# RWKV6 attention and a tanh-shrink feed-forward layer: joining a second pair of steps in blocks 3 to 5, with forms of weights kept in device memory

## The chip, the cores and the metric

The kernel runs on one core of a Trainium2 chip. The metric is the device time of one execution in microseconds (us). The engines are named as in the profile: PE (TensorE, matrix products, with PEld for its weight loads), DVE (VectorE), ACT (ScalarE), POOL (GpSimd) and SP (SyncE, which issues most DMAs). Each engine works through its own program in order; semaphores tie the programs together.

## The reference

```python
batch, n_heads, seq, head_dim = (4, 8, 768, 48)
for t in range(S):                       # attention, one state of 48 x 48 for each head
    cur = einsum('bhd,bhe->bhde', u[None] * k[t], v[t])
    y[t] = einsum('bhd,bhde->bhe', r[t], state + cur)
    state = w[t][..., None] * state + einsum('bhd,bhe->bhde', k[t], v[t])
x = y.transpose(0, 2, 1, 3).reshape(3072, 384)
h = x @ w_in                             # 384 -> 2048
g = h - tanh(h)
out = g @ w_out                          # 2048 -> 384
```

All inputs and outputs are float32.

## The kernel before

The 3072 tokens are cut into eight blocks of 384 (four batches, two halves each). A block is a loop over 16 steps `f` (L1355), each one slice of 128 of the 2048 inner features. While block i does its feed-forward layer, the attention of block i+1 (`later`) is prepared, and inputs of block i+2 (`after`) are loaded. PE, SP, DVE and ACT run in the order in which the code is written (`manual_schedule`), so that the position of a line is its place in the engine's queue.

**One single step.** `first` (L886) multiplies the block's tokens `xT` by the step's slice of `w_in`: three 128x128x384 products into the bank `hp`, which the profile shows as six rows of L888. ACT copies the result to `h` (L893). `slight` (L967) then has ACT form `s` (the square), `qa` and `junk` (a check of the range, called `over`), and leaves two products for DVE (L896), which run in the next step as `rest`. They give a slice of `g`.

**The second layer.** Two steps make a pair q. Its 384x256x384 product is done by `Fewer` (L1078) with fewer multiplications, from sums and differences of parts of g (`form_g`, L1009; DVE rows of L1013) and of `w_out`. `form_g` runs over the following steps: forms 0 and 2 as `formed`, 4, 6 and 8 as `forming`, or `carried` to a later step around a joined pair. The products of a pair go to PE in two parts (`Fewer.add`, twelve rows of L1092 each), the first two steps after the pair's end, the second three; the list `due` holds them. Three more products of each pair, `others` (L1106), go to a bank of `ps_a`; for pairs 0 to 3 that is in step 9. The pieces are put together in the next block by `SUMS` (DVE rows of L1127), in the steps that the dictionary `some` (L1388) names.

**A joined pair.** For the pairs in `JOINED` (L122) the two steps share their first product. `Twos.begin` (L938) makes it from 11 products of 128x128x192 (22 rows of L951) into the two tiles of `ps_a`. It needs five forms of the weights (`weight_forms`, L919, DVE rows of L927) and four forms of the tokens (`token_forms`, L930, DVE rows of L935). ACT copies one part out (L952), and four DVE additions (`outs`, rows of L961) give h of both steps. `begin` and `outs` stand in the even step; `slight` follows there for the first h, and in the odd step for the second. Blocks 3 to 6 join pair 1 (steps 2 and 3), block 6 also pair 7, block 7 pairs 0 to 6.

**Room on the chip.** The forms and results of a joined pair lie in tiles whose contents are not needed just then (`spare_tile`, L899): pair 1 uses `v_sb` and `late` for its forms and `ks` for its results. A tile taken this way is written only when its last reader is done.

**The attention of the next block**, by steps as `plan` (L1146) gives them for blocks 3 to 6: `split` (ACT) writes 16-bit planes into tile `w` in step 2; `turned` (L547) is a DMA transposition from `w`, in step 4 to `ks` and in step 5 to `post`; `join` (ACT rows of L555) puts the words together again in `ks`: one copy each in steps 6, 7 and 8, three in step 9. `update` (PE rows of L578, step 10) reads `ks`, in the order of head pairs 3, 2, 1, 0 for four chunks of tokens and then the same for the last two; the three copies of step 9 belong to head pairs 1 and 0. It is followed by the updates of the states on DVE (L590, step 11), and `results` (PE rows of L774, step 12). `product_u`, `product_r` and `product_sum` (DVE) stand in steps 5, 6 and 7, `diagonal_in` in 8 and 9. The loads of the block after next stand at steps 7 (`w`), 9 (`k`) and 11 (`r`); `bound` (ACT, L459) and `behind` (DVE scan) read the new `w` from step 10 on.

**DVE's order within a step** is one list, such as this one for the even step of a joined pair beyond the first:

```python
ops = between(rest, carried) + outs[:1] + formed + outs[1:] + spare
```

`between` interleaves two lists; `spare` holds the sums, the preparation of the next block and the forms for joined pairs.

Of the kernel before, what the change touches and what calls it, by code (L numbers as in the profile page):

```python
# [37 lines left out]
F32 = mybir.dt.float32  # L38
# [13 lines left out]
P = 128  # L52
L = 64
NB = 384
NQ = S // NB
NCH = NB // L
NCP = NCH // 2
NPAIR = H // 2
# [7 lines left out]
DM = H * D  # L66
FF = 2048
KC = DM // P
NF = FF // P
# [44 lines left out]
SUMS = (("sub", (15, 6, 10), (0, 0, 6)), ("sub", (2, 2, 5), (3, 5, 3)),  # L114
        ("add", (6, 7, 13), (1, 7, 1)), ("add", (7, 9, 14), (5, 9, 11)),
        ("sub", (10, 10, 14), (5, 5, 6)), ("add", (11, 12, 11), (10, 2, 10)),
        ("sub", (14, 4, 14), (11, 3, 11)), ("add", (2, 8, 13), (10, 5, 10)),
        ("add", (13, 4, 13), (2, 2, 15)), ("add", (8, 8, 12), (4, 4, 12)),
        ("add", (0, 4, 0), (11, 2, 11)), ("sub", (14, 14, 1)))
PLACES = ((8, 10, 0), (2, 5, 13), (11, 7, 14))  # L120
TWOS = range(7)
JOINED = {3: (1,), 4: (1,), 5: (1,), 6: (1, NF // 2 - 1), 7: TWOS}  # L122


SLIGHT = 2.0 ** -6
# [4 lines left out]
def kernel(  # L130
# [12 lines left out]
    nc = tc.nc  # L143
# [3 lines left out]
    work = ctx.enter_context(tc.tile_pool(name="work", bufs=2))  # L147
# [42 lines left out]
    def draw(names, cols):  # L190
        nc.gpsimd.memset(mask_all[0:L, cols], 1.0)
        for m in names:
# [5 lines left out]
            else:  # L198
# [10 lines left out]
                   in_=start[:, 0:BANK].unsqueeze(1).to_broadcast([P, 2 * NPAIR * NCP * L // BANK, BANK]))  # L209
# [107 lines left out]
    def begin_behind(ins, then):  # L317
        tc.add_manual_dep(then.ins, ins.ins.name, mybir.DependencyInfo(
            mybir.DependencyClass.Sync, mybir.DependencyReason.DATA))
# [579 lines left out]
    def spare_tile(name, width=2 * HALF, pool=inp):  # L899
        return pool.tile([P, width], F32, name=name, tag=name, bufs=1)  # L900
# [245 lines left out]
    def plan(i):  # L1146


        formed_w = {}
        if i == 0:  # L1150
            phases = {6: ("turn",), 7: ("update",), 10: ("earlier",), 13: ("results",)}
            before = {0: ("behind 2", "take_whole 2"), 2: ("behind 0", "take_whole 0"), 3: ("times_behind 2",),
                      4: ("times_behind 0",), 5: ("before 2",), 6: ("before 0",), 7: ("times_before",),
                      9: ("product_u", "held", "bound 2"), 10: ("product_r", "bound 0"), 11: ("product_sum",), 12: ("diagonal_in 2", "diagonal_in 0")}
            ahead = {}
            loads = {f: "weights" for f in (0, 1, 3, 4, 5, 6, 7, 8, 9, 10)}
            loads.update({2: "next r", 11: "w", 13: "k", 14: "r"})
            loads = {f: [name] for f, name in loads.items()}
            loads[3] += ["v", "row"]
            loads[4] += ["tokens k"]  # L1160
            loads[9] += ["tokens r"]
        else:
            phases = {3: ("split 2 0",), 4: ("earlier", "split 2 1", "turned 2", "split 0 01"), 5: ("turned 0",),
                      6: ("join 2 0",), 7: ("join 2 1",), 8: ("join 2 2",), 9: ("join 0 02",), 10: ("update",),
                      12: ("results",)}
            before = {0: ("times_behind 2",), 1: ("times_behind 0",), 3: ("times_before", "held"),
                      5: ("product_u",), 6: ("product_r",), 7: ("product_sum",), 8: ("diagonal_in 2",),
                      9: ("diagonal_in 0",)}
            ahead = {10: ("bound 2", "bound 0"), 11: ("behind 2", "take_whole 2"), 12: ("behind 0", "take_whole 0"),
                     13: ("before 2",), 15: ("before 0",)}  # L1170
            loads = {1: ["v"], 3: ["tokens k"], 4: ["tokens r"], 7: ["w"], 9: ["k"], 11: ["r"]}
            if i in JOINED:
                before.update({2: ("times_before",), 3: ("held",)})
                phases.update({3: (), 4: ("earlier", "turned 2")})
                loads = {3: ["tokens k"], 4: ["tokens r"], 5: ["v"], 7: ["w"], 9: ["k"], 11: ["r"]}
        if i == 1:
            phases = {4: ("split 2 0",), 5: ("split 2 1", "turned 2"), 6: ("split 0 01",),
                      7: ("earlier", "turned 0", "join 2 0"), 8: ("join 2 1",), 9: ("join 2 2", "join 0 01"),
                      10: ("join 0 2",), 11: ("update",), 13: ("results",)}
            before = {0: ("behind 2", "take_whole 2", "bound 2"), 1: ("behind 0", "take_whole 0"),  # L1180
                      2: ("times_behind 2",), 3: ("before 2", "bound 0"), 4: ("times_behind 0",), 5: ("before 0",),
                      6: ("times_before", "held"), 7: ("product_u",),
                      9: ("product_r", "product_sum", "diagonal_in 2"), 10: ("diagonal_in 0",)}
            ahead = {12: ("bound 2",), 13: ("behind 2", "take_whole 2"), 14: ("bound 0",)}
            loads = {1: ["v"], 4: ["tokens k"], 6: ["tokens r"], 9: ["w"], 11: ["k"], 12: ["r"]}
            formed_w = {2: (0, 1), 7: (2, 3, 4, 5), 9: (6,), 10: (7, 8), 11: (9,), 12: (0, 1), 13: (2, 3, 4, 5, 6),
                        14: (7, 8, 9)}
        elif i == 2:
            phases.update({3: (), 4: ("split 2 0",), 5: ("earlier", "split 2 1", "turned 2", "split 0 01"),
                           6: ("turned 0", "join 2 0")})  # L1190
            before = {0: ("behind 0", "take_whole 0", "times_behind 2"), 1: ("times_behind 0",), 2: ("before 2",),
                      3: ("before 0",), 4: ("times_before", "held"), 5: ("product_u",), 7: ("product_r",),
                      8: ("product_sum",), 9: ("diagonal_in 2", "diagonal_in 0")}
            loads = {1: ["v"], 3: ["tokens k"], 5: ["tokens r"], 8: ["w"], 10: ["k"], 11: ["r"]}
        return phases, before, ahead, loads, formed_w
# [1 line left out]
    blocks = [Block(b, q) for b in range(B) for q in range(NQ)]  # L1197
    manual = ExitStack()
    manual.enter_context(tc.manual_schedule(engines={PE, SP, DVE, ACT}))
    raws = []  # L1200

    def more_weights(queue):
        raws.append(load_weights(more_weights.n, queue))
# [141 lines left out]
    for i, blk in enumerate(blocks):  # L1345
        here = xT
# [8 lines left out]
        for f in range(NF):  # L1355
# [8 lines left out]
            if not joined:  # L1364
                h, made = first(here, f, to[:, 0:NB], SPACED[i][f > 12 + (i < 2)])
            elif f % 2 == 0:
                for op in behind:
                    op()
                behind = []
                by = beside if near else twos  # L1370
                outs = by.begin(ps_a, f // 2)
                if near:
                    for name in ("split 2 0", "split 2 1", "split 0 01"):
                        later.phase(ps_a, name)
            if not i:
# [9 lines left out]
                    op()  # L1385
            else:
                ahead_of_h, square = [], []
            some = ({4: (0, 2), 6: (2, 4), 8: (4, 6), 9: (6, 8), 14: (8, len(SUMS))} if after else  # L1388
                    {4: (0, 2), 6: (2, 4), 8: (4, 6), 9: (6, 8), 11: (8, 10), 12: (10, len(SUMS))} if later else
                    {4: (0, 1), 5: (1, 2), 6: (2, 3), 7: (3, 4), 8: (4, 5), 9: (5, 9), 10: (9, 11),  # L1390
                     11: (11, len(SUMS))}).get(f) if summed else None
# [4 lines left out]
                              if of and not name.startswith("bound")]  # L1396
            if i:
                spare += [lambda n=n: form_w(n, 4 if f < 12 else 6, 2) for n in formed_w.get(f, ())]
            if later and i in JOINED and f < 2:
                if not f:  # L1400
                    beside, v_left, late_left = (Twos(1, 1), spare_tile("v_sb", NCP * DM), spare_tile("late", NB))
                    for x in range(5):
                        beside.form(x, v_left, x * P)
                    beside.results(spare_tile("ks", NPAIR * NCP * P, work))
                    spare += beside.weight_forms(0, 2, 1, 4, 3)
                else:
                    spare += beside.token_forms(here, beside.halves((v_left, 5 * P), (late_left, 0)))
            if i == blocks_n - 2:
                if f == 10:
                    twos = Twos(0, NF // 2)  # L1410
# [107 lines left out]
            for name in loads.get(f, ()):  # L1518
                of, ins = (after if name in ("w", "k", "r") else later), None
                if name == "weights":  # L1520
                    ins = more_weights(nc.sync)
                elif name == "row":
                    ins = nc.sync.dma_start(out=u_row, in_=u_all)
                elif of and name.startswith("tokens"):
                    ins = of.load_tokens(name[-1])
                elif of:
                    ins = of.load_v() if name == "v" else of.load(name.split()[-1])
                if ins:
                    begin_behind(made, ins)
            if f < 2 and summed:  # L1530
                summed[0].others(ps_a, ((4, 5, 6), (7,))[f], None if later else hp)
                if f:
                    behind.append(summed[0].others_summed)
# [95 lines left out]
```

## Time and profile before

| | before |
|---|---|
| median of 3 runs | 541.09 us (540.89 to 542.05) |
| profiled execution, own time | 540.57 us |
| its span, first to last instruction | 538.7 us |
| PE clock granted in it | 0.998 |
| DVE groups: form_g L1013, sums L1127 | 106.6 us in 270, 33.0 us in 84 |
| ACT groups: qa L980, junk L984 | 69.6 us in 113, 68.0 us in 113 |
| DMA moved | 56.36 MB, mean 105 GB/s |

A row of a timeline gives start, duration, engine, line, operation, output and inputs, and how many instructions were merged; a bracket gives the idle time before it and what ended it. PE rows of a timeline overlap by about 0.16 us because products are pipelined; the chain that ended last gives them end to end. Two engine rows that overlap on DVE or ACT do so in the same way.

### The profile page before, as it was taken

How to read it: one execution, taken by the hardware profiler on the slowest of the kernel's cores; microseconds unless marked ns; L12 is line 12 of the kernel's file. 1: busy time of each engine (PE TensorE's matmuls, PEld its weight loads, DVE VectorE, ACT ScalarE, POOL GpSimd, SP SyncE). 2: the span in 40 equal slices, each digit the busy share in tenths (PEclk: the TensorE clock that was granted, in tenths of full speed). 3: DMA queues.
4: the chain of work that ended last, by engine and by line, in shares of the span. 5: the costliest groups of instructions: out<-in, count | busy, mean ns of one | idle time of the engine just before them, and what ended most of it. 6: DMA issues, size and time to landing. Idle time of an engine off the chain costs nothing.

```text
span 538.7 us, 15161 instructions
## 1 busy us (share of the span) xinstructions
PE 529.3 (98%) x5820; PEld 419.7 (78%) x5820; DVE 495.9 (92%) x1044; ACT 393.4 (73%) x796; POOL 9.2 (2%) x57
## 2 busy tenths in 40 slices
PE   7999999999999999999999999999999999999996
PEld 5756665677777777877878787787878877999993
DVE  7999999999989989999898989989899899979885
ACT  4999986988668876678676787587865886546460
POOL 1100000000000000000000000000000000000001
PEclk9999999999999999999999999999999999999999
DMA  8798742252311632164211632128232340100011
GB/s 279 244 408 327 237 122 72 101 136 65 121 32 65 163 109 59 53 116 150 63 56 46 149 119 66 51 60 192 63 90 68 47 103 16 43 2 1 10 36 47
DMA packets 53049, 56.36 MB, mean 105 GB/s; under 512 B 21488, under 2 KB 50928, under 8 KB 52976
## 3 DMA queue, kind: packets, MB, share of 16 engines
q1 hardware_dynamic: 52592, 55.18, 34.8%
q8 instruction: 49, 0.80, 0.6%
q14 instruction: 24, 0.20, 0.1%
q10 hardware_dynamic: 288, 0.10, 0.1%
q0 software_dynamic: 96, 0.07, 0.1%
HBM read 44.73 MB, written 4.72 MB: 92 GB/s over the span
## 4 chain that ended last, share of the span: by engine, by line
PE 95%; DVE 2%; DMA 1%; PEld 1%; issue 0%; ACT 0%; SPq 0%; PEldq 0%; DVEq 0%
PE hp L888 36%; PE acc L1092 27%; PE att L951 8%; PE att L1092 6%; PE acc L1043 5%; PE att L774 4%; PE att L497 2%; PE att L578 1%; PE acc L1070 1%; PE att L888 1%; DMA r<-in_rT 1%; PE acc L888 1%; PE hp L1092 0%; PE att L520 0%; DVE scores L505 0%; DVE pre L420 0%
## 5 line engine op out<-in xcount | busy, mean ns | idle before, releaser
L888 PE MATMUL hp<-xT,w_sb 128*128 128x384 f32 x594 | 208.8, 488 | 0.5 <-DVE w_sb L271 0.5
L888 PEld LDWEIGHTS hp<-xT,w_sb 128*128 128x128 f32 x594 | 106.3, 190 | 57.0 <-issue 0.6
L1092 PE MATMUL acc<-forms,g 128*128 128x128 f32 x972 | 136.0, 276 | 0.0
L1092 PEld LDWEIGHTS acc<-forms,g 128*128 128x128 f32 x972 | 124.4, 192 | 7.7
L1013 DVE TENSOR_TENSOR g<-g 128x256 f32<-128x256 f32 x270 | 106.6, 419 | 0.7 <-PE acc L1092 0.2
L893 ACT ACTIVATE h<-hp 128x384 f32<-128x384 f32 x99 | 48.5, 490 | 75.4 <-PE hp L888 75.3
L980 ACT ACTIVATE qa<-s,shift 128x384 f32<-128x384 f32 x113 | 69.6, 616 | 3.7
L984 ACT ACTIVATE junk<-s,shift 128x384 bf16<-128x384 f32 x113 | 68.0, 601 | 0.4
L896 DVE SCALAR_TENSOR_TENSOR h<-h,s 128x384 f32<-128x384 f32 x104 | 57.1, 549 | 11.7 <-ACT s L979 11.6
L1092 PE MATMUL acc<-w_sb,g 128*128 128x128 f32 x324 | 54.1, 276 | 0.0
L1092 PEld LDWEIGHTS acc<-w_sb,g 128*128 128x128 f32 x324 | 47.0, 192 | 7.6 <-ACT sums L1060 0.3
L896 DVE SCALAR_TENSOR_TENSOR g<-qa,h 128x384 f32<-128x384 f32 x88 | 48.4, 550 | 1.3
L979 ACT ACTIVATE s<-h 128x384 f32<-128x384 f32 x89 | 46.6, 523 | 2.8
L1127 DVE TENSOR_TENSOR sums<-sums 128x256 f32<-128x256 f32 x84 | 33.0, 409 | 1.2 <-ACT sums L1104 1.0
L1043 PE MATMUL acc<-w_sb,sums 128*128 128x384 f32 x96 | 33.7, 487 | 0.0
L1092 PE MATMUL att<-w_sb,g 128*128 128x128 f32 x200 | 33.4, 275 | 0.0
L267 ACT ACTIVATE up<-raw 128x768 f16<-128x768 f32 (+1 forms) x32 | 33.1, 1076 | 0.0
L1092 PEld LDWEIGHTS att<-w_sb,g 128*128 128x128 f32 x200 | 29.0, 192 | 4.2
L1043 PEld LDWEIGHTS acc<-w_sb,sums 128*128 128x128 f32 x96 | 18.0, 190 | 12.3 <-DVE sums L896 0.3
L420 DVE TENSOR_TENSOR_SCAN pre<-w,start 128x780 f32<-128x780 f32 x14 | 25.0, 1783 | 0.8
L951 PE MATMUL att<-xT,w_sb 128*128 128x192 f32 x120 | 25.4, 326 | 0.0
L432 DVE TENSOR_TENSOR_SCAN post<-w,seed 128x780 f32<-128x780 f32 x14 | 24.9, 1776 | 0.0
(185 smaller groups left out, 715.2 us busy)
## 6 DMA issues: line engine op xcount, KB each, us to landing
raw<-in_weights SPq DMA_DIRECT2D x16, 768.0 KB, 6.7
w<-in_wT SPq DMA_DIRECT2D x7, 780.0 KB, 4.5
k<-in_kT SPq DMA_DIRECT2D x7, 768.0 KB, 5.2
r<-in_rT SPq DMA_DIRECT2D x7, 768.0 KB, 4.6
v_sb<-in_v SPq DMA_DIRECT2D x8, 576.0 KB, 4.7
k<-in_tokens SPq DMA_DIRECT2D x7, 576.0 KB, 3.9
r<-in_tokens SPq DMA_DIRECT2D x7, 576.0 KB, 4.9
out_y<-sums SPq DMA_DIRECT2D x18, 128.0 KB, 1.9
```

The lines of the kernel that those rows point to most:

```text
L267: return lambda: nc.scalar.activation(out=to, in_=of, func=AF.Copy, scale=scale, bias=bias)
L888: nc.tensor.matmul(hp, lhsT=w_in_sb[:, f, kc, :], rhs=xT[kc], start=(kc == KC - 1), stop=(kc == 0))
L893: return h, nc.scalar.activation(out=h, in_=hp, func=AF.Copy, scale=1.0 / UPSCALE)
L896: return lambda: nc.vector.scalar_tensor_tensor(out=out, in0=in0, scalar=scalar, in1=in1, op0=op0, op1=ALU.mult)
L951: nc.tensor.matmul(to, lhsT=lhs, rhs=rhs, start=n == 0, stop=n + 1 == len(of))
L979: nc.scalar.activation(out=s, in_=h, func=AF.Square, scale=scale)
L980: nc.scalar.activation(out=qa, in_=s, func=AF.Square, bias=shift[:, 4:5])
L984: nc.scalar.activation(out=junk[:, 0:NB], in_=s, func=AF.Relu, bias=shift[:, 5:6], accum_out=excess[:, at:at + 1])
L1013: return lambda: nc.vector.tensor_tensor(out=G[:, to:to + 2], in0=two(G, g_at(q, a0), g_at(q, a1)), in1=two(G, g_at(q, b0), g_at(q, b1)), ...
L1043: nc.tensor.matmul(acc, lhsT=g[:, j * P:(j + 1) * P], rhs=w_out_sb[:, f, :], start=(f == self.first), stop=(f == NF - 1))
L1092: nc.tensor.matmul(to, lhsT=G[:, g_at(q, a), :], rhs=rhs, start=start, stop=stop, skip_group_check=True)
L1127: ops.append(lambda op=op, at=at: nc.vector.tensor_tensor(out=at[0], in0=at[1], in1=at[2], op=OPS[op]))
```

## The change

Blocks 3, 4 and 5 also join pair 4, steps 8 and 9. The five forms of weights of pairs 1 and 4 are made once, in step 10 of block 2, in the spare tile `r`, and stored to a buffer `kept` of 128 x 1280 floats in device memory. Blocks 3 to 6 load those of pair 1 into `v_sb` in step 14 of the block before, in place of making them in step 0. Blocks 3 to 5 load those of pair 4 into the spare tile `w` in step 5; the token forms of pair 4 are made in step 6, in the same tile `w`, and its results go to the spare tile `r`. The load of the next `w` moves from step 7 to step 8, the two `bound` from step 10 to 11, and the sums of steps 8 and 9, two each, to step 10.

```diff
-JOINED = {3: (1,), 4: (1,), 5: (1,), 6: (1, NF // 2 - 1), 7: TWOS}
+JOINED = {3: (1, 4), 4: (1, 4), 5: (1, 4), 6: (1, NF // 2 - 1), 7: TWOS}
+KEPT = (1, 4)
...
             if i in JOINED:
...
+                if 4 in JOINED[i]:
+                    loads.update({7: [], 8: ["w"]})
+                    ahead.update({10: (), 11: ("bound 2", "bound 0", "behind 2", "take_whole 2")})
...
-    raws = []
+    raws, besides = [], {}
+    kept = ctx.enter_context(tc.tile_pool(name="kept", bufs=1, space=bass.MemoryType.DRAM)).tile(
+        [P, 10 * P], F32, name="kept", tag="kept")
...
-                by = beside if near else twos
+                by = besides[f // 2] if later and f // 2 in besides else twos
                 outs = by.begin(ps_a, f // 2)
-                if near:
+                if f == 2 and near:
...
-            some = ({4: (0, 2), 6: (2, 4), 8: (4, 6), 9: (6, 8), 14: (8, len(SUMS))} if after else
+            some = ({4: (0, 2), 6: (2, 4), 10: (4, 8), 14: (8, len(SUMS))} if after and 4 in JOINED.get(i, ()) else
+                    {4: (0, 2), 6: (2, 4), 8: (4, 6), 9: (6, 8), 14: (8, len(SUMS))} if after else
...
-            if later and i in JOINED and f < 2:
-                if not f:
-                    beside, v_left, late_left = (Twos(1, 1), spare_tile("v_sb", NCP * DM), spare_tile("late", NB))
+            if i + 1 == min(JOINED) and f == 10:
+                left = spare_tile("r")
+                for q, at in zip(KEPT, (0, 5 * P)):
+                    makes = Twos(q, 1)
                     for x in range(5):
-                        beside.form(x, v_left, x * P)
-                    beside.results(spare_tile("ks", NPAIR * NCP * P, work))
-                    spare += beside.weight_forms(0, 2, 1, 4, 3)
-                else:
-                    spare += beside.token_forms(here, beside.halves((v_left, 5 * P), (late_left, 0)))
+                        makes.form(x, left, at + x * P)
+                    spare += makes.weight_forms(0, 2, 1, 4, 3)
+            if later and i in JOINED:
+                if f == 0:
+                    besides[1].results(spare_tile("ks", NPAIR * NCP * P, work))
+                elif f == 1:
+                    late_left = spare_tile("late", NB)
+                    spare += besides[1].token_forms(here, besides[1].halves((v_left, 5 * P), (late_left, 0)))
+                elif f == 6 and 4 in besides:
+                    spare = besides[4].token_forms(here, besides[4].halves((w_left, 5 * P), (w_left, 5 * P + NB))) + spare
+                elif f == 7 and 4 in besides:
+                    besides[4].results(spare_tile("r"))
...
+            if i + 1 == min(JOINED) and f == 10:
+                nc.sync.dma_start(out=kept, in_=left[:, 0:10 * P])
+            if f == 14 and i + 1 in JOINED and i + 2 < len(blocks):
+                besides = {1: Twos(1, 1)}
+                v_left = spare_tile("v_sb", NCP * DM)
+                nc.sync.dma_start(out=v_left[:, 0:5 * P], in_=kept[:, 0:5 * P])
+                for x in range(5):
+                    besides[1].form(x, v_left, x * P)
+            if f == 5 and later and 4 in JOINED.get(i, ()):
+                besides[4], w_left = Twos(4, 1), spare_tile("w")
+                nc.sync.dma_start(out=w_left[:, 0:5 * P], in_=kept[:, 5 * P:10 * P])
+                for x in range(5):
+                    besides[4].form(x, w_left, x * P)
```

## The prediction, made before the change was run

> **What bounds the kernel now.** I read the page's busy times first, then the chain that ended last, then the windows and the waits.
>
> ```profile
> PE 529.3 (98%) x5820; PEld 419.7 (78%) x5820; DVE 495.9 (92%) x1044; ACT 393.4 (73%) x796; POOL 9.2 (2%) x57
> ...
> PE 95%; DVE 2%; DMA 1%; PEld 1%; issue 0%; ACT 0%; SPq 0%; PEldq 0%; DVEq 0%
> ```
>
> TensorE (PE) is 98% busy and 95% of the chain. The question is whether it stays gapless in blocks 3 to 5, and that depends on the engine with the least room. So next come two windows: one block, and inside block 4 the stretch from step 4 to step 10. Columns: window, its length, then PE, PEld, DVE, ACT and POOL busy.
>
> ```profile
> 345.50:409.20 63.70, 63.70 (x717) 51.69 (x716) 59.27 (x130) 47.26 (x101) 0.32 (x4) 1.00 0.35 91
> 294.60:319.40 24.80, 24.80 (x232) 19.41 (x231) 24.48 (x51) 20.35 (x44) 0.00 (x0) 1.00 0.55 145
> ```
>
> PE has no hole in either. VectorE (DVE) has 4.4 us free in a block of 63.7, but only 0.3 us between 294.6 and 319.4: there it runs without a pause, and whatever is added delays all that follows. Its next real pause is in step 10 (start, duration, instruction, in brackets the idle time before it):
>
> ```profile
> 318.98 0.42 DVE L1013 TENSOR_TENSOR g<-g 128x256 f32<-128x256 f32 x1
> 321.58 0.56 DVE L896 SCALAR_TENSOR_TENSOR h<-h,s 128x384 f32<-128x384 f32 x1 [2.18 <-ACT s L979]
> ```
>
> The pair in question sits just before that pause. PE in steps 7 to 11 of block 4, from the chain in order of time (start, us, what):
>
> ```profile
> 309.30 1.94 PE hp L888 x6
> 311.24 1.34 PE acc L1092 x12
> 312.57 1.94 PE hp L888 x6
> 314.51 2.68 PE att L1092 x24
> 317.19 1.34 PE acc L1092 x12
> 318.53 1.94 PE hp L888 x6
> 320.47 1.22 PE att L578 x80
> 321.69 1.53 PE acc L1092 x12
> ```
>
> Step 8 is the first two rows. Step 9 is the next three, with `others` (att L1092) in the middle; step 10 starts at 318.53 and holds `update` (L578).
>
> **What it removes from PE.** A joined pair costs 3.58 us, as block 7 shows for the same pair 8 and 9:
>
> ```profile
> 497.47 3.58 PE att L951 x22
> ...
> 502.39 2.68 PE att L1092 x24
> ```
>
> Two single steps cost 2 x 1.94 = 3.88. The change saves 0.30 us a block, **0.9 us** in three. That is the whole possible gain I can find, since PE has no waits in these blocks for another edit to remove.
>
> **The forms of weights.** Block 2 makes ten at step 10; blocks 3 to 6 no longer make five each at step 0.
>
> ```profile
> L927 DVE TENSOR_TENSOR v_sb<-w_sb 128x128 f32<-128x128 f32 x12 | 3.4, 285 | 0.0
> ```
>
> Ten are at most 2.9 us. They land in the pause of block 2's step 10:
>
> ```profile
> 194.20 0.56 DVE L896 SCALAR_TENSOR_TENSOR h<-h,s 128x384 f32<-128x384 f32 x1 [1.62 <-ACT s L979]
> ```
>
> At most 1.3 us are left over. What they push back is the update of the states for `results` of step 12. In block 4 that update begins its last row at 327.19, and PE begins `results` at 329.77:
>
> ```profile
> 327.19 0.36 DVE L590 TENSOR_TENSOR states<-states,whole 128x192 f32<-128x192 f32 x1
> ```
> ```profile
> 329.77 2.83 PE att L774 x192
> ```
>
> That is 2.2 us of room, taken as the same in block 2. I cost the ten at nothing; without that cover they cost 1.3 us. The five that leave step 0 free DVE there, but PE did not wait for them, and in step 4 DVE waits for ScalarE (ACT) again. I count no gain.
>
> **The DMAs.** The 640 KB store of `kept` sits on SP ahead of block 2's load of r, which is not read until step 2 of block 3, seven steps on: nothing. The loads for pair 1 go out at step 14, four steps ahead: nothing. The load for pair 4 goes out in step 5, behind the transposition `post<-w` that still reads tile w, and behind v. The trace has no such load of 320 KB. Bounds are the 1.9 us of a 192 KB store and the 5.4 us of block 3's v load of 576 KB:
>
> ```profile
> out_y<-o SPq DMA_DIRECT2D x2, 192.0 KB, 1.9
> ...
> v_sb<-in_v SPq DMA_DIRECT2D x1, 576.0 KB, 5.4
> ```
>
> I take 3.0 us, nearer the small one. Issued at 305.3 in block 4 (the landing of `post<-w`, below) it lands at 308.3; PE begins the pair at 309.30 and wants the first form after six of its 22 rows, at 310.3. In block 3 the transposition lands 1.0 us later against the step, and 1.0 us of room is left. At 5.4 us PE would wait 1.4 us there, mostly time that it loses below anyway: 0.5 us at the far end, nothing at the near one. The Trainium skill, "DMA: Bandwidth & Descriptors", section "Anatomy of one DMA", gives 2.0 us plus bytes over 436 GB/s for another issue path; as an estimate that is 2.8 us here, and the load would be in time. The loads of w and k for the block after next go out a little later or earlier, well ahead of their first readers.
>
> **What it adds to DVE.** Four forms of tokens at step 6, four `outs` at step 8; two sums leave step 8 and two leave step 9 for step 10, into the pause.
>
> ```profile
> 286.01 0.35 DVE L935 TENSOR_TENSOR v_sb<-xT 128x192 f32<-128x192 f32 x1
> 286.28 0.35 DVE L935 TENSOR_TENSOR late<-xT,xT 128x192 f32<-128x192 f32 x1
> ...
> 291.75 1.41 DVE L961 TENSOR_TENSOR ks<-ks,att 128x384 f32<-128x384 f32 x3 [0.39 <-PE att L951]
> ```
>
> The token forms start 0.27 apart: 1.1 us. Three `outs` take 1.41 us; I count 0.47 for a wide one, like the products further down, and 0.28 for the narrow third.
>
> But the first token form writes into tile w, and must wait until `post<-w` has read it. The token form takes the place after the first `h<-h,s` of step 6, where the first sum starts now. Issue and landing in blocks 3, 4, 5, with that place:
>
> ```profile
> 236.60 2.19 SPq L549 DMA_TRANSPOSE post<-w  x1
> ...
> post<-w SPq DMA_TRANSPOSE x1, 6.1
> ```
> ```profile
> 241.07 0.41 DVE L1127 TENSOR_TENSOR sums<-sums 128x256 f32<-128x256 f32 x1
> ```
> ```profile
> 304.26 0.55 DVE L896 SCALAR_TENSOR_TENSOR h<-h,s 128x384 f32<-128x384 f32 x1
> 304.73 0.41 DVE L1127 TENSOR_TENSOR sums<-sums 128x256 f32<-128x256 f32 x1
> ```
> ```profile
> 300.22 2.00 SPq L549 DMA_TRANSPOSE post<-w  x1
> ...
> post<-w SPq DMA_TRANSPOSE x1, 5.1
> ```
> ```profile
> 368.45 0.42 DVE L1127 TENSOR_TENSOR sums<-sums 128x256 f32<-128x256 f32 x1
> ```
> ```profile
> 363.97 2.42 SPq L549 DMA_TRANSPOSE post<-w  x1
> ...
> post<-w SPq DMA_TRANSPOSE x1, 5.5
> ```
>
> The landings are at 242.7, 305.3 and 369.5, so DVE waits 1.6, 0.6 and 1.0 us. Queued behind that wait is everything of steps 6 to 9. DVE enters step 8 late by 1.1 + 0.6 = 1.7 us in block 4 (2.7 in block 3, 2.1 in block 5).
>
> **What is late next, block 4.** DVE begins step 8 now with this row:
>
> ```profile
> 311.01 0.55 DVE L896 SCALAR_TENSOR_TENSOR h<-h,s 128x384 f32<-128x384 f32 x1
> ```
>
> With 1.7 us more and the two products (0.47 each, the distance from 304.26 to 304.73 above), the first `outs` runs 313.65 to 314.2. PE is done with the pair and its 1.34 us of products at 309.30 + 3.58 + 1.34 = 314.22 and goes to `others`, which overwrites the bank that this `outs` reads: no more than about 0.2 us of refill is lost in block 4 (1.53 against 1.34 above, where PE changes over), but 0.6 in block 5 and 1.2 in block 3. The third `outs`, which completes the first h, ends at 313.65 + 0.47 + 0.33 + 0.47 + 0.35 = 315.3 (0.33 is a form of g, 0.42 long with 0.09 overlapped; 0.35 is the length of a 192-wide row). Only then can ACT begin both steps' activations, and the copies that `update` needs stand behind them in its program:
>
> ```profile
> 294.05 0.53 ACT L979 ACTIVATE s<-ks 128x384 f32<-128x384 f32 x1
> ...
> 297.53 0.47 ACT L893 ACTIVATE h<-hp 128x384 f32<-128x384 f32 x1
> ```
> ```profile
> 317.23 0.49 ACT L1104 ACTIVATE o<-att 128x384 f32<-128x384 f32 x1 [0.38 <-PE att L1092]
> 317.61 2.01 ACT L555 COPY ks<-post 128x512 uint16<-128x512 uint16 x3
> ```
>
> The first fence is the existing pair's two activations, 3.48 us. Add one join copy (0.67), the scaling (0.38) and the three copies (2.01): 315.3 + 6.54 = 321.8, where they end at 319.6 now. The last quarter of `update` needs the last copy, so `update` ends near 322.1 in place of 321.69: **+0.4 us** in block 4 with the saving already in it. Each later microsecond of DVE adds as much: +0.8 in block 5, +1.4 in block 3. The sum is 2.6 us. DVE then restarts in step 11 about 1 us later relative to PE, and `results` have the 2.2 us of room, so nothing more is added.
>
> Against the profiled execution's own 540.57 us that is 543.2; its time is 0.5 below the median of the runs, 541.09, so the forecast is **543.7**.
>
> **The rivals.** (1) *PE alone counts*, the other side: the lag stays under the point from which it decides. `update` would end unstalled at 321.4, so that point is a DVE lag of 1.3 us in place of 1.7, 2.1 and 2.7. Then the result is -0.9: 540.2. For it: block 7's `others` follows the same pair at 502.39 without a gap. Against it: that stretch has no transposition, joins or update. The Trainium skill, "Perfetto Trace Analysis", section "Identifying Performance Opportunities", says that a kernel improves with its most-contended engine; by that rule this rival wins, and the trace agrees only as far as PE's 98%. (2) *No wait on the transposition*: it lands before DVE gets there. The lag is 1.1, ACT's copies end at 321.2, and each block gives 0.2 back: 540.5. Against it: three landings out of three are late. (3) *The lag runs on*: the load for pair 4 is at its far end, and `results` or the next block's pair waits for DVE too, about 0.8 us a block more: 546.1. Against it: the 2.2 us of room there, and the 1 us that step 0 loses.
>
> **How the numbers follow.** Forecast 0.68, rival 1 0.14, rival 2 0.10, rival 3 0.08. About what a measurement of this kernel can tell from no change is 0.2%, here 1.1 us: 540.0 to 542.2. Faster needs rival 1 with 0.2 us more than its rows: 0.06. Same takes the rest of rivals 1 and 2 and the forecast's low edge: 0.22. Slower: 0.72. The forecast's own range, with landings 0.5 us either way in each block, is 542.0 to 545.3; the range of 8 in 10 reaches to rival 1 and toward rival 3: 540.3 to 545.6.
>
> **What would show it.** Right: a DVE idle of 0.6 to 1.6 us before the first token form in step 6, ended by the transposition; a PE gap before `others` in block 3 above all; a PE gap inside L578 ended by ACT's copies; the step from pair to step 10 differing between blocks as the landings do. Wrong: blocks 3 to 5 each 0.3 us shorter, PE without gaps, or a stall at L951 for a load.

## The result, and the profile after

The changed kernel takes 546.81 us (median of 6 runs, 546.20 to 550.85), the kernel before in the same comparison 541.51 (540.89 to 542.27): a ratio of 1.0104, 95% interval 1.0074 to 1.0133, or 5.3 us slower. The forecast was 543.7, its range ended at 545.6. Lines of the code carry a number one higher than before (L1093 is the old L1092, L936 the token forms, L962 the `outs`, L579 `update`). The profiled execution is the slowest of the six, 550.85 us, with a span of 549.0; the last section takes up why.

First the page's busy times and its chain by engine:

```profile
PE 534.7 (97%) x5850; PEld 428.4 (78%) x5850; DVE 504.2 (92%) x1058; ACT 390.4 (71%) x793; POOL 9.2 (2%) x57
...
PE 81%; DVE 6%; ACT 5%; DMA 4%; issue 2%; PEld 0%; SPq 0%; PEldq 0%; DVEq 0%
```

By busy share little has changed: PE 97% in place of 98%. The chain says otherwise: 81% of it is PE in place of 95%, and DVE, ACT and a DMA have the rest. Windows from the start of pair 1 (step 2) to the start of pair 1 in the next block show where. First the kernel before, then the changed one (window, length, busy PE, PEld, DVE, ACT, POOL, then the granted PE clock):

```profile
224.31:287.97 63.66, 63.66 (x717) 51.65 (x716) 59.02 (x128) 47.23 (x101) 0.32 (x4) 1.00 0.36 91
287.97:351.69 63.72, 63.72 (x716) 51.71 (x715) 59.09 (x129) 47.23 (x101) 0.32 (x4) 1.00 0.33 91
351.69:415.35 63.66, 63.66 (x716) 51.65 (x715) 59.23 (x128) 47.22 (x101) 0.32 (x4) 1.00 0.36 91
```

```profile
226.17:293.40 67.23, 65.25 (x726) 54.65 (x725) 61.53 (x131) 46.33 (x100) 0.32 (x4) 0.97 0.38 96
293.40:358.79 65.39, 64.08 (x727) 53.26 (x726) 61.62 (x132) 46.05 (x100) 0.32 (x4) 1.00 0.37 98
358.79:425.88 67.09, 65.25 (x726) 54.64 (x725) 61.54 (x131) 46.29 (x100) 0.32 (x4) 0.97 0.38 96
```

Blocks 3, 4 and 5 are 3.57, 1.67 and 3.43 us longer, and PE is idle in each for the first time: 1.98, 1.31 and 1.84 us (length less busy). In blocks 3 and 5 the clock is 0.97 as well; that is taken up at the end.

The waits (engine, what, what ended the wait; total, times, longest) name the same chain as the prediction:

```profile
ACT s L980 <- DVE r L962: 17.2, 3, 6.0
...
DVE w L936 <- DMA post<-w: 5.0, 3, 2.0
PE att L1093 <- DVE r L962: 4.9, 3, 2.0
```

Per block: DVE waits for the transposition before the first token form, PE waits for DVE's first `outs` before `others`, ACT waits for the first h. No wait at L952 for the loads of `kept` appears; in the list of DMA issues those for pair 4 land in 2.8 to 3.0 us (3.0 had been assumed). The transpositions, in blocks 3, 4 and 5 (KB and us to landing):

```profile
post<-w SPq DMA_TRANSPOSE x1, 6.6
...
post<-w SPq DMA_TRANSPOSE x1, 5.6
...
post<-w SPq DMA_TRANSPOSE x1, 6.4
```

They take 0.5, 0.5 and 0.9 us more than the 6.1, 5.1 and 5.5 of before. Now block 4 on DVE, from step 6 to the `outs` of step 8 (start, duration, instruction, idle before it):

```profile
309.68 0.57 DVE L897 SCALAR_TENSOR_TENSOR h<-h,s 128x384 f32<-128x384 f32 x1
311.34 0.36 DVE L936 TENSOR_TENSOR w<-xT 128x192 f32<-128x192 f32 x1 [1.09 <-DMA post<-w]
...
312.68 0.75 DVE L936 TENSOR_TENSOR w<-xT,w 128x192 f32<-128x192 f32 x2
313.35 0.88 DVE L1128 TENSOR_TENSOR sums<-sums 128x256 f32<-128x256 f32 x2
314.14 1.35 DVE L390 TENSOR_TENSOR k<-k,r 128x1152 f32<-128x1152 f32 x1
...
317.69 1.35 DVE L394 TENSOR_REDUCE diagonal<-k 128x24 f32<-128x1152 f32 x1
318.95 0.55 DVE L897 SCALAR_TENSOR_TENSOR h<-h,s 128x384 f32<-128x384 f32 x1
319.61 0.56 DVE L897 SCALAR_TENSOR_TENSOR g<-qa,h 128x384 f32<-128x384 f32 x1
320.08 0.55 DVE L962 TENSOR_TENSOR r<-r,att 128x384 f32<-128x384 f32 x1
320.55 0.42 DVE L1014 TENSOR_TENSOR g<-g 128x256 f32<-128x256 f32 x1
320.88 1.40 DVE L962 TENSOR_TENSOR r<-r,att 128x384 f32<-128x384 f32 x3
```

And on PE in the same block, its pair and the two rows that carry a gap:

```profile
314.57 1.14 PE L952 MATMUL att<-xT,w_sb 128*128 128x192 f32 x6
...
320.68 0.49 PE L1093 MATMUL att<-w_sb,g 128*128 128x128 f32 x2 [1.04 <-DVE r L962]
...
327.77 1.01 PE L579 MATMUL att<-v_sb,ks 64*48 64x48 f32 x40 [0.27 <-ACT ks L556]
```

The second gap is preceded by the lateness that DVE hands to ACT. In order of time, the chain that ended last:

```profile
321.46 0.36 DVE r L962
...
321.85 0.53 ACT s L980
...
326.44 1.30 ACT ks L556 x2
...
327.77 1.01 PE att L579 x40
```

The third `outs` releases the activations of both steps, and the copies for `update` come out behind them. Both places were named in the prediction; both are later than it said.

### The profile page after: what moved, and what is told of

It reads as the page before. It is cut to its first block, busy times and chain, and to the rows that moved or that the text cites. A ratio compares the mean times of both kernels' runs of the same rounds, so it can differ in the third digit from the quotient of the medians.

```text
span 549.0 us, 15208 instructions
## 1 busy us (share of the span) xinstructions
PE 534.7 (97%) x5850; PEld 428.4 (78%) x5850; DVE 504.2 (92%) x1058; ACT 390.4 (71%) x793; POOL 9.2 (2%) x57
## 4 chain that ended last, share of the span: by engine, by line
PE 81%; DVE 6%; ACT 5%; DMA 4%; issue 2%; PEld 0%; SPq 0%; PEldq 0%; DVEq 0%
PE hp L889 29%; PE acc L1093 22%; PE att L952 8%; PE att L1093 6%; PE acc L1044 5%; PE att L775 4%; DMA post<-w 3%; PE att L498 1%; PE att L579 1%; ACT junk L985 1%; PE acc L1071 1%; ACT qa L981 1%; PE att L889 1%; ACT s L980 1%; DMA r<-in_rT 1%
## 5 line engine op out<-in xcount | busy, mean ns | idle before, releaser
L889 PE MATMUL hp<-xT,w_sb 128*128 128x384 f32 x558 | 196.1, 488 | 0.5 <-DVE w_sb L272 0.5
L889 PEld LDWEIGHTS hp<-xT,w_sb 128*128 128x128 f32 x558 | 99.9, 190 | 53.8 <-issue 0.5
L1093 PE MATMUL acc<-forms,g 128*128 128x128 f32 x972 | 135.9, 276 | 0.0
L1093 PEld LDWEIGHTS acc<-forms,g 128*128 128x128 f32 x972 | 124.3, 192 | 6.9
L894 ACT ACTIVATE h<-hp 128x384 f32<-128x384 f32 x93 | 45.5, 489 | 74.6 <-PE hp L889 74.6
L897 DVE SCALAR_TENSOR_TENSOR h<-h,s 128x384 f32<-128x384 f32 x98 | 54.1, 552 | 3.8 <-ACT s L980 3.5
L1093 PE MATMUL acc<-w_sb,g 128*128 128x128 f32 x324 | 54.1, 276 | 0.0
L1093 PEld LDWEIGHTS acc<-w_sb,g 128*128 128x128 f32 x324 | 47.1, 192 | 7.6 <-ACT sums L1061 0.3
L897 DVE SCALAR_TENSOR_TENSOR g<-qa,h 128x384 f32<-128x384 f32 x82 | 45.3, 552 | 0.9
L980 ACT ACTIVATE s<-h 128x384 f32<-128x384 f32 x83 | 43.5, 524 | 2.6
L1093 PE MATMUL att<-w_sb,g 128*128 128x128 f32 x200 | 36.0, 291 | 4.9 <-DVE r L962 4.9
L1093 PEld LDWEIGHTS att<-w_sb,g 128*128 128x128 f32 x200 | 31.2, 207 | 8.9 <-DVE r L962 5.4
L952 PE MATMUL att<-xT,w_sb 128*128 128x192 f32 x150 | 31.8, 326 | 0.0
L952 PEld LDWEIGHTS att<-xT,w_sb 128*128 128x128 f32 x150 | 24.9, 190 | 0.0
```

Source lines behind the costliest of these rows:

```text
L889: nc.tensor.matmul(hp, lhsT=w_in_sb[:, f, kc, :], rhs=xT[kc], start=(kc == KC - 1), stop=(kc == 0))
L894: return h, nc.scalar.activation(out=h, in_=hp, func=AF.Copy, scale=1.0 / UPSCALE)
L897: return lambda: nc.vector.scalar_tensor_tensor(out=out, in0=in0, scalar=scalar, in1=in1, op0=op0, op1=ALU.mult)
L952: nc.tensor.matmul(to, lhsT=lhs, rhs=rhs, start=n == 0, stop=n + 1 == len(of))
L980: nc.scalar.activation(out=s, in_=h, func=AF.Square, scale=scale)
L1093: nc.tensor.matmul(to, lhsT=G[:, g_at(q, a), :], rhs=rhs, start=start, stop=stop, skip_group_check=True)
```

## The experiments

Theory A is the prediction's mechanism with larger sizes: DVE is late by its wait on the transposition and by its added work; PE pays before `others`, and again inside `update`, where ACT's copies stand behind the late activations. The rivals are those that each expectation names. Eight runs were made, in two groups of four; beside the first group the kernel before took 540.95 us (23 runs), beside the second 541.4 (29 runs).

**1. The forms without the pair.** Pair 4 is not joined; the ten forms, the store, the loads for pair 1 stay.

```diff
-JOINED = {3: (1, 4), 4: (1, 4), 5: (1, 4), 6: (1, NF // 2 - 1), 7: TWOS}
+JOINED = {3: (1,), 4: (1,), 5: (1,), 6: (1, NF // 2 - 1), 7: TWOS}
```

> The forms of both pairs are made in block 2, stored and loaded for pair 1, but pair 4 is not joined. Theory A (the whole loss is the lag of DVE and ACT around pair 4): no PE gap in blocks 2 to 6, 541.5 us, within 0.5 of before. Rival C (the ten forms in block 2, the store or the loads cost something, or they are what makes the transposition post<-w land later): 542.5 or more, or landings of 5.6 to 6.6 us as in the changed kernel in place of 5.1 to 6.1.

Measured: 540.85 us, ratio 1.0001 (0.9990 to 1.0013). PE is busy without a hole around the places that matter (windows in blocks 3 and 4):

```profile
240.00:270.00 30.00, 30.00 (x409) 23.99 (x411) 27.49 (x57) 23.84 (x50) 0.32 (x4) 1.00 0.48 133
305.00:335.00 30.00, 30.00 (x424) 23.90 (x423) 27.45 (x59) 23.17 (x50) 0.32 (x4) 1.00 0.41 116
```

The forms in block 2, the store and the loads for pair 1 cost nothing that can be measured, as forecast: the whole loss comes with pair 4. Its three blocks take 63.66, 63.73 and 63.66 us. The transpositions land after 6.6, 5.6 and 5.6 us in this kernel too, which is the other sign that rival C named: their later landing does not need pair 4, and costs nothing where no row of DVE waits for it. In block 4 runs 2 and 3 have the same forms, store and loads and land after 5.1 us, as before; in block 3 every profile with them has 6.5 or 6.6. What the later landing comes from stays open.

**2. Other work for PE ahead of `others`.** In step 9 the first part of pair 3's products (twelve rows of L1093) goes ahead of `others`, so that PE has 1.34 us of work while DVE finishes the first `outs`.

```diff
+                if joined and later:
+                    add_due(now)
```

> The changed kernel, with PE's six products of pair 3 (1.34 us) ahead of others in step 9, so that the first outs has 1.34 us more before PE needs its bank. Theory A (two limits in series: the first outs, and right behind it ACT's copies for update, which end 8.2 us after the first outs begins): the gap before others falls from 1.97, 1.04 and 1.84 to about 0.6, 0 and 0.5, but update then waits for the copies by about the same, 546.0 to 546.8. Rival B (others is the only limit): 3.4 us less, 543.4.

Measured: 546.94 us, ratio 1.0106 (1.0087 to 1.0125), no gain at all, and just above the range of theory A. The waits show why:

```profile
PE acc L1093 <- DVE g L1014: 2.5, 3, 1.4
...
PE att L579 <- ACT ks L556: 1.8, 6, 0.3
```

These products need the second form of g, and DVE makes it just behind the first `outs`: PE now waits for that row instead. What it gains there it gives back inside `update`, with two waits of 0.3 us in each block, since ACT's copies are no earlier. The order on PE is not the cause; DVE's and ACT's lateness is.

**3. ACT's copies earlier.** The four copies of steps 8 and 9 that `update` needs (`join 2 2` is one, `join 0 02` three) are issued in step 8, ahead of the activations that wait for DVE.

```diff
+                    phases.update({8: (), 9: ()})
...
+                if f == 8 and later:
+                    for name in ("join 2 2", "join 0 02"):
+                        later.phase(ps_a, name)
```

> The changed kernel, with ACT's four join copies of steps 8 and 9 moved up, right behind the copy in begin, into ACT's idle time of 6 us. Theory A: the gaps before others stay at 1.0 to 2.0, only the 0.3 us gap inside update in block 4 goes, 546.2 to 546.6. Rival D (ACT's copies set the pace of steps 8 to 10 in all three blocks): 543 to 544.

Measured: 544.88 us (543.86 to 546.94), ratio 1.0076 (1.0052 to 1.0100): between the two expectations. About 1.5 us of the loss is gone. The gap inside `update` is gone from the trace, the one before `others` is not:

```profile
DVE w L936 <- DMA post<-w: 4.1, 3, 2.0
PE att L1093 <- DVE r L962: 3.9, 3, 2.0
```

Theory A had priced the copies at the visible gap of 0.3 us in block 4 alone. But `update` as a whole takes 1.94 us there (326.84 to 328.78) in place of 1.29 before, so the late copies cost 0.65 us, and not in block 4 alone: the gap inside `update` is also there in blocks 4 and 5 of run 8, and in all three blocks of run 2, where PE's first gaps are 1.42, 0.32 and 0.76 us. It is missing where the first gap is followed by half the clock (last section), so that PE reaches `update` later.

**4. No wait on the transposition.** The token forms of pair 4 go to the free end of tile `k` and to `late`. They are made in the same place in DVE's order, but write to nothing that the transposition reads.

```diff
-                    spare = besides[4].token_forms(here, besides[4].halves((w_left, 5 * P), (w_left, 5 * P + NB))) + spare
+                    tails = (later.tile("k"), NCP * DM), (spare_tile("late", NB), 0)
+                    spare = besides[4].token_forms(here, besides[4].halves(*tails)) + spare
```

> The changed kernel, with the token forms of pair 4 in the unused end of tile k and in tile late, so that they need not wait for the transposition that reads tile w. Theory A: no DVE idle in step 6, DVE's lag at step 8 falls from 3.4, 2.5 and 3.3 to about 1.4 us, the gap before others to 0.2 or nothing, and the copies cost 0.3 to 0.5 us a block: 542.0 to 543.0. Rival B (others the only limit): 541.0. Rival C (DVE's added work, not the wait, is the price): 545 or more.

Measured: 542.89 us, ratio 1.0032 (1.0019 to 1.0045). That is 1.9 us above the kernel before in place of about 5.5: the wait is two thirds of the loss. One wait is left among those of PE in these blocks, ACT's copies:

```profile
PE att L579 <- ACT ks L556: 0.8, 3, 0.3
```

With it a block is 0.48 us longer than before (64.14, 64.20, 64.14 us). The gap of 0.26 us is the visible part; `update` is also cut in two by it, and in the chain of this kernel it ends 0.65 us later against the pair's start than in run 5 below.

**5. Both.** Runs 3 and 4 together, with the same four copies as in run 3 (the expectation says three).

> The token forms of pair 4 go to the end of tile k and to tile late, so that they need not wait for the transposition, and three of ACT's copies for `update` (join 2 2 and join 0 02) are issued in step 8, ahead of the activations of the joined pair. Theory A (the three blocks lose time by two chains only: DVE's wait on the transposition, and ACT's copies behind the two activations): no PE gap is left in blocks 3 to 5, each is 0.3 us shorter than before the change, 63.4 us from pair to pair in place of 63.7; the time is 540.0 to 540.4 beside a kernel before of 541.0. Rival E (the four token forms and four additions on DVE alone make DVE too late, and the gap comes back before `others` or before the first products of the pair): 541.5 to 542.5. Rival F (the copies moved forward make the activations of step 8 late, and with them DVE's products and forms): a gap of 0.2 to 0.5 us a block before the first products of step 10, 541.0 to 542.0.

Measured: 540.49 us, ratio 0.9987 (0.9977 to 0.9998). From pair to pair:

```profile
224.97:288.45 63.48, 63.48 (x726) 53.03 (x725) 60.91 (x131) 46.20 (x100) 0.32 (x4) 1.00 0.40 101
288.45:352.00 63.55, 63.55 (x727) 53.09 (x725) 61.09 (x131) 46.19 (x100) 0.36 (x4) 1.00 0.37 102
352.00:415.48 63.48, 63.48 (x727) 53.02 (x726) 61.38 (x132) 46.21 (x100) 0.32 (x4) 1.00 0.38 101
```

PE has no hole left, as theory A expected, and each block is 0.17 to 0.18 us shorter than before the change, not 0.30. The chain in block 4 holds the difference, in the piece that is `others`:

```profile
314.70 2.79 PE att L1093 x24
```

`others` takes 2.79 us in place of 2.68. The first `outs` ends at 314.50 here (313.95 and 0.55 long on DVE), 0.05 before `others` begins on the timeline. PE shows no idle time there, so that these 0.11 us are spent refilling it is a reading; that they hang on the first `outs` is what run 6 shows. Of rival E no more than this is seen, of rival F nothing.

**6. Less on DVE before the pair.** As run 5, and three rows of DVE go one step later.

```diff
+                    before.update({7: (), 8: ("product_sum",), 9: ("diagonal_in 2",), 10: ("diagonal_in 0",)})
```

> As the run above, and product_sum goes from step 7 to step 8, one diagonal_in from step 8 to 9 and the other from 9 to 10: about 1 us less on DVE ahead of the pair's additions. Theory A: no gap was left to remove, so the time is the same as above within 0.3 us. Rival E: DVE's lag was what was left, and this run is 0.5 to 1.5 us faster than the one above.

Measured: 540.40 us, ratio 0.9982 (0.9967 to 0.9996). In the medians that is run 5 again. In the trace the first `outs` ends at 313.41, `others` takes 2.68 us, and the first of the three blocks is this long:

```profile
225.26:288.63 63.37, 63.37 (x727) 52.95 (x726) 60.80 (x131) 46.20 (x100) 0.32 (x4) 1.00 0.41 102
```

So the saving of 0.30 us a block is there once neither DVE nor ACT is late: 63.66 less 63.37 is 0.29. This kernel and run 5 beat the kernel before by 0.18% and 0.13%; both intervals end just below 1.

**7. One block alone.** Pair 4 is joined in block 4 only.

```diff
-JOINED = {3: (1, 4), 4: (1, 4), 5: (1, 4), 6: (1, NF // 2 - 1), 7: TWOS}
+JOINED = {3: (1,), 4: (1, 4), 5: (1,), 6: (1, NF // 2 - 1), 7: TWOS}
```

> The changed kernel with pair 4 joined in block 4 alone; blocks 3 and 5 keep the steps of before, with their forms loaded. Theory A (each block pays by its own, through its own transposition): block 4 is 1.7 us longer than before, blocks 3 and 5 as before, 542.5 to 542.9 beside 541.0. Rival G (what a block pays runs on into the next, so that one block alone pays less than its share of 5.3): below 542.0. Rival H (a gap's price is mostly the half clock after it): block 4's gap of 1.0 us gives no half clock, and the time is within 0.5 us of 541.0 in most runs.

Measured: 543.32 us (541.82 to 545.10), ratio 1.0038 (1.0025 to 1.0051), so 1.4 to 2.8 us. The profiled execution is the fastest of the twelve, 541.82. In it the blocks are:

```profile
224.36:288.02 63.66, 63.66 (x716) 51.68 (x715) 58.16 (x123) 47.22 (x101) 0.32 (x4) 1.00 0.39 96
288.02:353.19 65.17, 64.08 (x726) 53.28 (x725) 61.60 (x132) 46.02 (x100) 0.32 (x4) 1.00 0.36 99
353.19:416.85 63.66, 63.66 (x716) 51.68 (x715) 58.19 (x123) 47.23 (x101) 0.32 (x4) 1.00 0.37 96
```

Block 4 alone pays 1.45 us (65.17 less 63.72), its neighbours nothing: a block pays by its own transposition, and nothing runs on. By the medians it is 1.9 us (543.32 less 541.4), with the 1.5 to 1.9 that theory A expected above the kernel before; rivals G and H asked for at most 1.0 and 0.5.

**8. The changed kernel again**, for a second profiled execution; nothing is edited.

> The changed kernel once more, for a second profiled execution. Theory A: the time is 546.2 to 547.2; PE's gap before `others` in each of blocks 3, 4 and 5 is within 0.3 us of what the landing of that block's transposition gives (about the landing less 4.6 us in blocks 3 and 4, and less 4.5 us in block 5), whatever the landing is in this execution. Rival H (half clock after a gap): a gap of 1.5 us or more inside one stretch of 3.41 us is followed by 3.4 us of half clock, a shorter one is not, and the profiled execution is 1.7 us longer for each.

Measured: 547.00 us (546.05 to 547.78), ratio 1.0103 (1.0086 to 1.0121). The transpositions land after 6.6, 5.5 and 5.6 us this time, and the gap before `others` follows each:

```profile
252.37 0.49 PE L1093 MATMUL att<-w_sb,g 128*128 128x128 f32 x2 [2.01 <-DVE r L962]
...
318.52 0.49 PE L1093 MATMUL att<-w_sb,g 128*128 128x128 f32 x2 [0.89 <-DVE r L962]
...
383.93 0.49 PE L1093 MATMUL att<-w_sb,g 128*128 128x128 f32 x2 [1.05 <-DVE r L962]
```

The landing less 4.6 (4.5 in block 5) gives 2.0, 0.9 and 1.1. Block 5 is the telling one: 6.4 us of landing in the first profile went with a gap of 1.84, 5.6 us in this one with 1.05.

## Why the prediction was wrong in size and right in direction

**Right.** The mechanism: DVE's idle before the first token form ended by the transposition, the PE gap before `others` largest in block 3, the gap inside `update` ended by ACT's copies, block 4 hurt least. Also right: nothing for the forms, the store and the loads (run 1), 3.0 us for the load of pair 4, 0.30 us of PE saved by a join (run 6). Rival 1 (PE alone counts, 540.2) needed a DVE lag under 1.3 us; it is 2.5 in block 4. PE at 97% does not show that 14 points of the chain had gone to others. The rule of the Trainium skill that was cited for it ("Perfetto Trace Analysis", section "Identifying Performance Opportunities"), that a kernel improves with its most-contended engine, does not speak for rival 1 either: the same section calls matmul busy time a poor measure and names the busy share of the weight loads among the better ones. That share is 78% here beside DVE's 92%, so that by this measure DVE is the most contended. Rival 3 (the lag runs on into the next block) falls with run 7.

**Wrong: the size of DVE's lag at step 8**, put at 2.7, 1.7 and 2.1 us in blocks 3, 4 and 5. In block 4 it is 2.5: from the h of step 6 to `diagonal` of step 7 the rows above take 317.69 - 309.68 = 8.01 us, those of before 309.75 - 304.26 = 5.49. Its terms:

| block 4, us | predicted | measured |
|---|---|---|
| wait on the transposition | 0.6 | 1.19 (311.34 less the slot of h, 309.68 + 0.47) |
| four token forms | 1.1 | 1.21 (the last two, one feeding the other, take 0.67 to the next row) |
| the two sums, now side by side | 0 | 0.12 (0.79 in place of 0.67) |
| lag at step 8 | 1.7 | 2.52 |

The wait was too small in each block: 1.6, 0.6 and 1.0 predicted, and DVE idle for 2.04, 1.09 and 1.90 us in the first profile, 2.08, 0.96 and 1.11 in the second. The prediction took the landings of one execution as they were. The six landings of the changed kernel seen since were all later, by 0.1 to 0.9 us, where the prediction had allowed 0.5 either way.

**Wrong next: what follows the lag.** In step 8 a sum used to stand between h and g; it had moved to step 10. Now g depends on the row just ahead of it and starts 0.66 us after h, in place of the 0.47 that was counted. The first `outs` starts 5.51 us after the pair (320.08 less 314.57), where the prediction's 313.65 lay 4.51 after the pair's 309.14 on the timeline: 0.8 from the lag, 0.2 from this order. So `others` waits 1.04 us in block 4 where "no more than about 0.2" was lost, and 1.97 and 1.84 in blocks 3 and 5 where 1.2 and 0.6 were.

**The path over ACT** was put at 6.54 us from the third `outs` to the end of the copies; on ACT's timeline in block 4 of run 4, where nothing waits for the transposition, the first activation and the last three copies stand like this:

```profile
316.60 0.52 ACT L980 ACTIVATE s<-r 128x384 f32<-128x384 f32 x1 [4.12 <-DVE r L962]
...
321.08 2.02 ACT L556 COPY ks<-post 128x512 uint16<-128x512 uint16 x3
```

321.08 + 2.02 - 316.60 = 6.5: the step held.

**The larger part of the miss is there without the wait.** Rival 2 priced a kernel without it at 540.5, 0.2 us back in each block. Run 4 is that kernel: each block is 0.48 us longer, and the medians say 1.9 us slower in place of 0.6 faster. So some 2.0 us (by the blocks) to 2.5 us (by the medians) of the 2.7 by which the forecast was short do not come from the wait; the wait itself costs 3.6 us (5.5 less 1.9) where the forecast had 3.2 (2.6 slower with it, 0.6 faster without). In block 4 of the first profile the two parts are nearly even: 0.6 us of the 1.27 missed there is the wait. Block 4 of run 4, on DVE and at PE's pair:

```profile
305.61 0.57 DVE L897 SCALAR_TENSOR_TENSOR h<-h,s 128x384 f32<-128x384 f32 x1
...
312.44 1.35 DVE L394 TENSOR_REDUCE diagonal<-k 128x24 f32<-128x1152 f32 x1
...
314.83 0.55 DVE L962 TENSOR_TENSOR r<-r,att 128x384 f32<-128x384 f32 x1
```
```profile
310.51 1.14 PE L952 MATMUL att<-xT,w_sb 128*128 128x192 f32 x6
```

The lag is 312.44 - 305.61 - 5.49 = 1.34 us, past the point of 1.3 on its own, where 1.1 had been counted. With the order of h and g the first `outs` starts 4.32 us after the pair, 0.4 later than the prediction's terms without the wait give (4.51 less 0.6). The third `outs` ends 0.14 us later against the first than was counted, because it reads the second and starts 0.59 us behind it, and `update` ends 0.43 us behind the copies in place of 0.3. Together that is the 0.7 us between 0.2 back and 0.48 lost.

So the step that failed is DVE's arrival at the pair's additions: its wait was taken from one execution, and its rows were priced as if none had to wait for the one ahead of it.

**The sum.** Predicted +1.4, +0.4 and +0.8 for blocks 3, 4 and 5, together 2.6. Measured in the first profile +3.57, +1.67 and +3.43; without the half clock of the next section, worth 1.7 each in blocks 3 and 5, it is +1.87, +1.67 and +1.73, together 5.3. That this is the difference of the medians is in part luck: at half clock the wait inside `update` is gone as well, so that 1.7 is too much to take off. Block 4 was the most wrong: its forecast lag of 1.7 stood 0.4 past the point of 1.3 from which DVE's lag costs time, the lag of 2.5 stands 1.2 past it.

## What to carry to other kernels

When an added instruction reuses a buffer, list who still reads the buffer and when that reader ends over several executions; a landing that varies by most of a microsecond, as these do, is a range in the sum, not a number. On an engine without pauses, count an inserted row at its place in the order: rows that used to separate two dependent instructions were hiding a distance (0.66 us from h to g here, in place of 0.47). A join that saves 0.3 us of PE is worth having only if the engine that feeds it and the engine that comes after it are both given the time: here another buffer and earlier copies turned 1.0% slower into 0.1 to 0.2% faster.

## What the hardware showed that was not expected

**A PE gap of 2 us can cost half the clock for 3.4 us more.** Windows of the first profile of the changed kernel, the gap in block 3 and what follows it (PEclk is the first figure after the POOL column):

```profile
252.42:254.39 1.97, 0.00 (x0) 0.00 (x0) 1.87 (x5) 0.00 (x0) 0.00 (x0) 1.00 0.92 325
254.80:258.20 3.40, 3.40 (x18) 3.40 (x17) 3.26 (x7) 2.58 (x5) 0.00 (x0) 0.50 0.64 219
```

The granted clock is 0.50 for 3.4 us, worth 1.7 us of PE time, and the same follows the gap of 1.84 us in block 5. A third such stretch lies at the start of the kernel. At 1.7 each that would be 5.1 us; this execution took 4.0 us more than the median. Half the clock is not what makes the changed kernel slower: the two of its six runs with a granted clock of 1.0 took 546.20 and 546.89 us. In the second profile the gap of 2.01 us in block 3 is followed by it, the 0.89 and 1.05 of blocks 4 and 5 are not. Run 3 had a gap as long with no drop behind it:

```profile
251.60:253.57 1.97, 0.00 (x1) 0.00 (x1) 1.87 (x5) 0.00 (x0) 0.00 (x0) 1.00 0.92 325
253.57:257.00 3.43, 3.43 (x30) 3.43 (x31) 3.29 (x8) 2.20 (x5) 0.00 (x0) 1.00 0.76 263
```

In the first profile the half-clock stretches begin at 22.7, 254.8 and 387.9 us, 68 and 39 times 3.413 us apart. On the grid that this gives, the gaps of 1.97 and 1.84 us each lie inside one cell of 3.413 us, and the 2.01 us of the second profile lie inside the cell that ends where its drop begins, at 253.6. The gap of run 3 lies across two: in that execution the clock falls only behind the last products, at 542.8 us, and 85 cells earlier a boundary is at 252.7. The Trainium skill, "TensorE: Matmul & The Clock Gate", Part 1, has a free-running window of 3413 ns, which these rows bear out; it puts the limit at an idle gap of more than about 3.4 us, and here 1.84 us was enough. Where the limit lies was not tried; in the uneven work of the kernel's first 25 us the clock dropped behind a gap of 1.03 us in one execution (run 4) and not behind 1.27 in another (run 6).

**The landing of a transposition wanders.** The same transposition from `w` to `post` landed in 5.2 to 6.4 us in block 5 over the ten profiles, in 5.1 to 5.6 in block 4, and in block 3 in 6.1 before the change and 6.5 or 6.6 in all nine profiles since.
